# Softmax sums on GpSimd, routing products and early lo parts on VectorE, new TensorE costs in the planner

## The chip, the cores and the metric

One core of a Trainium2 chip runs the kernel. Its engines work side by side, each through its own list of instructions in order: TensorE (PE; its weight loads are shown apart as PEld), VectorE (DVE), ScalarE (ACT), GpSimd (POOL) and SyncE (SP), which here issues transfers. The metric is the device time of one execution in microseconds, the median of several. The profile comes from one further execution, and all times read from it count from the start of its span.

## What is computed

Attention over 4 batches of 8 heads with 576 rows of 64 numbers, causal in blocks of 64 rows; its output, 2304 rows of 512, goes through a mixture of 8 experts with two chosen for each row, and then through a second one with one chosen for each row.

```python
# attention, per batch and head (S = 576, D = 64)
scores = q @ k.T / sqrt(64);  scores[block_i < block_j] = -1e9     # blocks of 64
attn = exp(scores - scores.max(-1))
attn = attn / (attn.sum(-1) + 1e-9)
x = (attn @ v) -> [2304, 512]
# first mixture (E = 8, F = 1024)
logits = x @ w_gate + log1p(exp(x @ w_noise)) * noise
top2, top2_w = the two largest of 8, softmax over them
out[mask] += top2_w * (relu(x[mask] @ w1[e]) @ w2[e])              # for each expert e
# second mixture
logits = x @ w_gate + modality_bias[modality_id];  e_idx = argmax
out[mask] = gate_w * (relu(x[mask] @ w1[e]) @ w2[e])
```

All inputs and outputs are 32-bit floats.

## The kernel before, in words

Every matmul of the large products is done in three passes of a rounded 32-bit type: an operand is split into a high part (a copy with rounding, ScalarE) and a low part (the rest, a subtraction). For the weights these tiles are called wh and wl (from raw, the loaded tile; kld, qld and other attention buffers serve as raw for the earliest), for rows of x xth and xtl, for the hidden layer hh and hl (kept in tiles kp), for the attention's probabilities PTh and PTl.

**Attention** runs in 16 pairs, each of two heads of one batch (`NPAIR`). The steps of a pair have names: T and K/Q (transposes and splits of q and k), S0 to S8 (scores, TensorE, banks ps), M (row maxima nm, VectorE), E (exponentials p with their sums ss, ScalarE), B (transposes of p on TensorE, banks pt), H and L (PTh and PTl), V (values, banks pa), C, X and XC (transposes back into xu, ScalarE). R, R1 and R2 make the factors of the rows: R adds the two halves of the last sum (1 column), R1 adds 1e-9 to all nine, R2 takes four reciprocals of at most 5 columns into rr; all three are VectorE's. GpSimd multiplies finished rows by them (x and LH, from xu and rr, of an earlier pair) and splits v (vs: a copy and a subtraction). Where nothing else is said, a step stands once in a pair.

What sets the order there is a planner at build time. The table `SCHED` (L19) gives a pair's length, 14.5 us, and for each step a due time in it. The loop takes, among the next steps of TensorE, ScalarE and VectorE whose predecessors (`before`, L1220) are done by the planner's own clocks, the one that can start first, within 0.15 us the one due first. The clocks run by costs: `dve_cost`, `pe_cost` (L83 to L91), `act_cost`, `pool_cost`, and a lag from one engine to the next (`lag`, L1216). A step of GpSimd is not in these lists; it is emitted behind the step that makes it ready.

**Routing** of the first mixture (`route`, L643) is a chain of small VectorE steps that is laid between the attention's steps (`aside`): after pair 7 and after pair 11 for two parts of the rows, after pair 15 for the last. It makes one-hot tables (`hot_b`, `hot_a`, L284; tiles sl_ob, sl_oa, and their product sl_ov with five values for each slot) which a matmul sums into lists of rows (`lists`, L295); `slot_ids` turns these into the row numbers by which an indirect DMA gathers each expert's rows. A flag `early` stands for the lists of the first experts, `ids1` for all. `hot_a` is given the engine for its product: GpSimd for the first two routings (128x2000 each), VectorE for the last.

**The first expert's first weights** are split while attention still runs (`Stage.split`, called at fixed times 110, 124, ... plus 11 us; and steps JS of the hidden layer behind the last pair, two of four on GpSimd). Then `run` goes through the experts: `mm1` for each of eight blocks of the hidden layer (banks ph), `mm2` for each 128 rows (banks py), and between them one split of the next expert's weights each (lists `ea` and `eb` say on which engine), the transposes of the next rows (px, xth, xtl), the rows' transfers and a `filler`, which carries out what is left of the routing. VectorE's dots of the rows with the gate weights of the second mixture (zero, from yr or py and wgb) make the next gate.

A helper class (`Timed`) records every operation, so each row of the trace carries its line, L71; tiles tell the rows apart.

The names that the change touches: `pe_cost` L83, `hot_a` L284, `lists` L295, `Stage.split` L450, `route` L643, R, R1 and R2 L975 to L990, `last_route` and `routes` L1127 to L1140, `S_` L1183, `OFF`, `engine`, `lag` and `before` L1206 to L1223, `emit` L1259, `earliest` L1280, the splits at fixed times L1309, `run` L1372.

Of the kernel before, what the change touches and what calls it, by code (L numbers as in the profile page):

```python
# [30 lines left out]
def moe_kernel(tc, q, k, v, w_gate, w_noise, noise, w1, w2, mod_id, w_gate2, mod_bias, m2w1, m2w2, out):  # L31
# [54 lines left out]
    def pe_cost(name, o, i, kw):  # L86
        n = cols_of(o)
        dt = i.dtype
        if name == "transpose":
            return n * .00084  # L90
        return 2 * max(cols_of(i) * .00084, n * .00084) if dt == F32 else n * .000417 + .0145 * (clk["base"] is None)  # L91
# [12 lines left out]
    with ExitStack() as top:  # L104
# [177 lines left out]
        made = [0]  # L282

        def hot_a(pool, a, n, a0, na, vals, eng):  # L284
# [5 lines left out]
            eng.tensor_tensor(ov, bc(oa[:, :, None, :], [128, n, NV, na]), bc(vals[:, :, :, None], [128, n, NV, na]), op=OP.mult)  # L290
            made[0] = clk["pool"] if eng is gps else 0
            yield .3
            return ov

        def lists(pl, ob, ov, n, first=True, last=True):  # L295
            yield "pe", made[0]
# [134 lines left out]
        class Stage:  # L431
# [18 lines left out]
            def split(s, eng):  # L450
# [5 lines left out]
                for x, raw in enumerate(parts):  # L456
                    act.activation(hi[:, m * x:m * x + m], raw, AF.Copy)
                    eng.tensor_sub(lo[:, m * x:m * x + m], raw, hi[:, m * x:m * x + m].bitcast(F32))
# [184 lines left out]
        def route(b0, nb, slow):  # L643
# [99 lines left out]
            for b in range(nb):  # L743
                n = slice(10 * b, 10 * b + 10)
                ob = yield from hot_b(rt, bl[:, n], 10)
                ov = yield from hot_a(rt, a[:, n], 10, 0, NA1, va[:, n], gps if slow else vec)
# [38 lines left out]
        with ExitStack() as ph:  # L785
# [70 lines left out]
            def pair(p):  # L856
# [118 lines left out]
                def R():  # L975
                    vec.tensor_add(st["ss"][:, 8:9], st["ss"][:, 8:9], st["ss"][:, 9:10])

                def R1():
                    vec.tensor_scalar(st["ss"][:, 0:9], st["ss"][:, 0:9], 1e-9, None, op0=OP.add)
# [12 lines left out]
                f.update(S8=S8, M8=M8, N8=N8, E8=E8, R=R, R1=R1, R2=R2)  # L992
# [134 lines left out]
            def last_route():  # L1127
                yield from route(B - 1, 1, False)
# [6 lines left out]
            def routes(i):  # L1135
                if i < 2:
                    yield from route((B - 2) * i, B - 2 - i, True)
# [7 lines left out]
            def first_steps():  # L1145
# [37 lines left out]
                def S_(i):  # L1183
                    stage.split(vec if i in (2, 3) else gps)
                    fetch_b(1)
# [21 lines left out]
            OFF.update(N8=OFF["M8"] + .1, R1=OFF["R"] + .1, R2=OFF["R"] + .2)  # L1207
            kinds = dict(T="pe", M="pe", H="act", R="act", S="act", L="dve", V="dve")

            def engine(n):  # L1210
                if n[0] == "J":
                    return kinds[n[1]]
                if n[0] in "TSBV" or n in ("X0", "X1"):
# [3 lines left out]
            lag = {"pe": .26, "act": .15, "dve": .13}  # L1217
# [4 lines left out]
                      "R": E_, "BT": ["E8"], "HT": ["BT"], "LT": ["HT"], "VX": ["L0", "VS"], "CX": ["VX"], "V0": L_ + ["VS"], "V1": L_ + ["VS"],  # L1222
# [443 lines left out]
```

## Time and profile before

| | us |
|---|---|
| median of 3 runs | 1021.34 (1020.36 to 1021.66) |
| profiled execution, whole time | 1020.32 |
| its span in the profile | 1018.5 |
| TensorE busy | 960.6 (94%) |
| VectorE busy | 733.8 (72%) |
| GpSimd busy | 528.5 (52%) |
| ScalarE busy | 519.0 (51%) |
| mean granted clock of TensorE | 0.985 of full |

The span is cut into stretches by what runs in it. From 30 to 144 us it is attention alone, from 144 to 265 attention with routing steps between, from 265 to 292 the hidden layer of expert 0, from 292 to 320 its second layer and the beginning of expert 1, from 320 to 400 the rest of expert 1, and from there the other experts of the first mixture, its gate and the second mixture. In a table of stretches each engine has its busy time and, in brackets, its number of instructions; a stretch less the busy time is the engine's idle time there. In a timeline the first number is the start, the second the length, then engine, line, operation, output <- inputs with their shapes, and at the end in square brackets the idle time ahead of it and whose instruction ended it. Instructions of one group that follow each other are put together (x4), and a group's length is then that of all.

### The profile page before, as it was taken

The page shows a single profiled execution, that of the slowest core. Times are in us where ns is not written, and L with a number is a line of the kernel's source. Part 1 is how long each engine was busy: PE and PEld are TensorE (multiplying, and loading weights), DVE is VectorE, ACT ScalarE, POOL GpSimd, SP SyncE. Part 2 cuts the span into 40 slices and gives each one's busy share as a digit, 9 for nine tenths or more (in the row PEclk, how much of TensorE's full clock was granted, in tenths as well). Part 3 has the DMA queues.
Part 4 walks back from the last instruction along what each step waited for, and adds up shares of the span by engine and source line. Part 5 has one row for each costly group of instructions (what it writes and reads, how often), then busy time and mean ns, then how long its engine had stood idle before and what let it go on. Part 6 is the DMA issues. An engine that isn't in the chain of part 4 may idle for free.

```text
span 1018.5 us, 17480 instructions
## 1 busy us (share of the span) xinstructions
PE 960.6 (94%) x6058; PEld 867.4 (85%) x6058; DVE 733.8 (72%) x1766; ACT 519.0 (51%) x1156; POOL 528.5 (52%) x387
## 2 busy tenths in 40 slices
PE   7999998898996999999999999999999989999995
PEld 5888887788886888998989898998979878999995
DVE  6888779989878596839396775939799876545541
ACT  5888887878653234433334333333325455555551
POOL 5123142373265649968485775847477345333231
PEclk8999999999997999999999999999999999999998
DMA  5556644322055636656374654625177867766620
GB/s 124 110 148 180 190 112 112 83 70 87 24 188 145 197 62 169 165 136 135 90 149 104 134 122 118 125 77 92 45 187 187 272 206 237 228 214 230 196 98 12
DMA packets 158257, 141.59 MB, mean 139 GB/s; under 512 B 76233, under 2 KB 124745, under 8 KB 158034
## 3 DMA queue, kind: packets, MB, share of 16 engines
q1 hardware_dynamic: 140098, 107.18, 35.6%
q0 software_dynamic: 18064, 33.23, 15.8%
q8 instruction: 50, 0.82, 0.4%
q14 instruction: 45, 0.37, 0.1%
HBM read 112.54 MB, written 28.36 MB: 138 GB/s over the span
## 4 chain that ended last, share of the span: by engine, by line
PE 74%; DVE 13%; issue 4%; ACT 3%; POOL 2%; DMA 2%; SPq 1%; POOLq 0%; DVEq 0%; ACTq 0%
PE ph L71 29%; PE py L71 25%; PE pt L71 8%; PE ps L71 6%; PE pa L71 4%; PE px L71 2%; POOL wl L71 1%; DVE ss L71 1%; DVE kp L71 1%; DVE zero L71 1%; DVE nm L71 1%; DVE PTl L71 1%; DMA wgb<-WG2T 1%; DMA xr<-X,ids 1%; DVE wl L71 1%
## 5 line engine op out<-in xcount | busy, mean ns | idle before, releaser
L71 POOL TENSOR_TENSOR wl<-raw,wh 128x1024 fp32r<-128x1024 f32 x88 | 226.8, 2624 | 112.4 <-ACT wh L71 98.2
L71 PE MATMUL ph<-xth,wh 128*128 128x320 f32 (+2 forms) x800 | 243.1, 304 | 12.5 <-DVE kp L71 12.5
L71 PE MATMUL ph<-xtl,wh 128*128 128x320 f32 (+2 forms) x800 | 241.9, 302 | 0.0
L71 PE MATMUL ph<-xth,wl 128*128 128x320 f32 (+2 forms) x800 | 241.8, 302 | 0.0
L71 DVE SCALAR_TENSOR_TENSOR zero<-py,gts,wgb 128x512 f32<-128x512 f32 x304 | 227.5, 748 | 8.6 <-issue 0.4
L71 PE MATMUL py<-wh,kp 128*128 128x512 f32 x496 | 166.9, 397 | 0.0
L71 PEld LDWEIGHTS ph<-xth,wh 128*128 128x128 f32 x800 | 153.3, 192 | 14.1 <-DVE kp L71 13.4
L71 PEld LDWEIGHTS ph<-xtl,wh 128*128 128x128 f32 x800 | 153.3, 192 | 0.7
L71 PEld LDWEIGHTS ph<-xth,wl 128*128 128x128 f32 x800 | 153.3, 192 | 0.0
L71 ACT ACTIVATE wh<-raw 128x1024 fp32r<-128x1024 f32 x144 | 150.8, 1053 | 0.7 <-DMA raw<-in_moe_w_dram 0.7
L71 ACT ACTIVATE yr<-py,gts 128x512 f32<-128x512 f32 x60 | 41.3, 689 | 147.0 <-PE py L71 104.4
L71 PEld LDWEIGHTS py<-wh,kp 128*128 128x128 f32 x496 | 93.3, 188 | 18.2
L71 DVE SCALAR_TENSOR_TENSOR hl<-ph,hh 128x320 fp32r<-128x320 f32 (+2 forms) x100 | 46.5, 466 | 80.6 <-ACT hh L71 80.3
L71 PE MATMUL ps<-kh,kp 128*128 128x256 f32 (+5 forms) x320 | 98.6, 349 | 2.5 <-POOL kp L71 1.0
L71 PE MATMUL py<-wl,kp 128*128 128x512 f32 x248 | 96.8, 391 | 0.0
L71 PE MATMUL py<-wh,hh 128*128 128x512 f32 x232 | 94.0, 405 | 0.0
L71 PE MATMUL py<-wl,hh 128*128 128x512 f32 x232 | 90.7, 391 | 1.4 <-POOL wl L71 1.4
L71 DVE TENSOR_TENSOR xtl<-px,xth 128x512 fp32r<-128x512 f32 x58 | 40.0, 690 | 71.3 <-ACT xth L71 71.0
L71 PE MATMUL py<-wh,hl 128*128 128x512 f32 x232 | 90.9, 392 | 0.0
L71 ACT ACTIVATE hh<-ph 128x320 fp32r<-128x320 f32 (+2 forms) x100 | 41.8, 418 | 95.4 <-PE ph L71 92.2
L71 POOL DMA_INDIRECT xr<-X,ids x55 | 58.1, 1057 | 62.2 <-PE px L71 47.4
L71 DVE TENSOR_TENSOR wl<-raw,wh 128x1024 fp32r<-128x1024 f32 x56 | 70.0, 1259 | 27.8 <-ACT wh L71 27.6
(252 smaller groups left out, 1861.4 us busy)
## 6 DMA issues: line engine op xcount, KB each, us to landing
raw<-in_moe_w_dram SPq DMA_DIRECT2D x144, 512.0 KB, 4.2
X<-zero SPq DMA_DIRECT2D x13, 512.0 KB, 3.6
kld<-in_k_dram SPq DMA_DIRECT2D x32, 128.0 KB, 2.7
qld<-in_q_dram SPq DMA_DIRECT2D x32, 128.0 KB, 2.8
vld<-in_v_dram SPq DMA_DIRECT2D x32, 128.0 KB, 2.7
X<-x SPq DMA_DIRECT2D x16, 256.0 KB, 2.3
xs<-in_moe_w_dram SPq DMA_DIRECT2D x4, 512.0 KB, 4.2
wgb<-WG2T POOLq DMA_DIRECT2D x1, 2048.0 KB, 9.0
```

The lines of the kernel that those rows point to most:

```text
L71: return f(*a, **kw)
```

## The change

- **Sums.** R adds both halves of the last sum and then 1e-9 to all nine, on GpSimd (R1 is gone). It is emitted as soon as the last exponential of its pair is. R2, the reciprocals, takes the due time that R had, and waits for R with the lag of GpSimd, 0.3 us.
- **Routing.** The product sl_ov is VectorE's in every routing, in two halves where it has more than 200 columns of one-hots. `lists` no longer reckons with GpSimd's clock.
- **Early lo parts.** The lo parts of weights that are split in attention buffers (`pre`) are written in halves of 512 columns. The first expert's lo parts are VectorE's, and in `run` all of them until the slot table of all experts (`ids1`) is there; from then on the lists `ea` and `eb` hold as before.
- **Planner's costs.** A 32-bit matmul costs 0.224 us whatever its size, a matmul of the rounded type its columns by 0.417 ns and 13.5 ns more (attention had no such addition, later stages had 14.5 ns), a transposed column 0.85 ns rather than 0.84. The table of due times itself is unchanged.

The core of the diff; what is left out passes on the same arguments or edits the table `before` so that R2 stands behind R.

```diff
@@ -87,8 +87,8 @@
         if name == "transpose":
-            return n * .00084
-        return 2 * max(cols_of(i) * .00084, n * .00084) if dt == F32 else n * .000417 + .0145 * (clk["base"] is None)
+            return n * .00085
+        return .224 if dt == F32 else n * .000417 + .0135
...
-        def hot_a(pool, a, n, a0, na, vals, eng):
+        def hot_a(pool, a, n, a0, na, vals):
...
-            eng.tensor_tensor(ov, bc(oa[:, :, None, :], [128, n, NV, na]), bc(vals[:, :, :, None], [128, n, NV, na]), op=OP.mult)
-            made[0] = clk["pool"] if eng is gps else 0
-            yield .3
+            m = -(-n // 2) if n * na > 200 else n
+            for c in range(0, n, m):
+                s = slice(c, min(c + m, n))
+                vec.tensor_tensor(ov[:, s], bc(oa[:, s, None, :], [128, s.stop - c, NV, na]),
+                                  bc(vals[:, s, :, None], [128, s.stop - c, NV, na]), op=OP.mult)
+                yield .3
             return ov
 
         def lists(pl, ob, ov, n, first=True, last=True):
-            yield "pe", made[0]
+            yield "pe", 0
...
-                    eng.tensor_sub(lo[:, m * x:m * x + m], raw, hi[:, m * x:m * x + m].bitcast(F32))
+
+                    k = 512 if parts[0] is pre else m
+                    for c in range(0, m, k):
+                        d = slice(m * x + c, m * x + c + k)
+                        eng.tensor_sub(lo[:, d], raw[:, c:c + k], hi[:, d].bitcast(F32))
...
-                ov = yield from hot_a(rt, a[:, n], 10, 0, NA1, va[:, n], gps if slow else vec)
+                ov = yield from hot_a(rt, a[:, n], 10, 0, NA1, va[:, n])
...
                 def R():
-                    vec.tensor_add(st["ss"][:, 8:9], st["ss"][:, 8:9], st["ss"][:, 9:10])
-
-                def R1():
-                    vec.tensor_scalar(st["ss"][:, 0:9], st["ss"][:, 0:9], 1e-9, None, op0=OP.add)
+                    gps.tensor_add(st["ss"][:, 8:9], st["ss"][:, 8:9], st["ss"][:, 9:10])
+                    gps.tensor_scalar(st["ss"][:, 0:9], st["ss"][:, 0:9], 1e-9, None, op0=OP.add)
...
                 def S_(i):
-                    stage.split(vec if i in (2, 3) else gps)
+                    stage.split(vec)
...
-            OFF.update(N8=OFF["M8"] + .1, R1=OFF["R"] + .1, R2=OFF["R"] + .2)
+            OFF.update(N8=OFF["M8"] + .1, R2=OFF.pop("R"))
...
+                if n in ("R", "VS"):
+                    return "pool"
...
-            lag = {"pe": .26, "act": .15, "dve": .13}
+            lag = {"pe": .26, "act": .15, "dve": .13, "pool": .3}
...
-                fin[p, n] = clk["pool" if n == "VS" else engine(n)]
+                fin[p, n] = clk[engine(n)]
+                if n in E_ and all((p, x) in fin for x in E_):
+                    emit(p, "R", t)
...
-                at(110 + 14 * i + 11, lambda: stage.split(gps))
+                at(110 + 14 * i + 11, lambda: stage.split(vec))
...
-                        stage.split(eb[fs.index(f) % len(eb)])
+                        stage.split(eb[fs.index(f) % len(eb)] if "ids1" in flags else vec)
...
-                            stage.split(ea[left[1] % len(ea)])
+                            stage.split(ea[left[1] % len(ea)] if "ids1" in flags else vec)
```

What this moves is read from the order of the instructions on each engine, at three places.

VectorE in the fourth pair, from the last split of the keys (kp) on. Before, the sums (ss) and the reciprocals (rr) stand ahead of PTh:

```order
L71 SCALAR_TENSOR_TENSOR kp_158<-pt,kp_156 64x8x64 x2
L71 TENSOR_TENSOR ss<-ss 128x1
L71 TENSOR_SCALAR ss<-ss 128x9
L71 RECIPROCAL rr_161<-ss 64x5
L71 RECIPROCAL rr_161<-ss 64x4
L71 RECIPROCAL rr_161<-ss 64x5
L71 RECIPROCAL rr_161<-ss 64x4
L71 TENSOR_TENSOR PTh<-pt,PTh 64x128
L71 TENSOR_REDUCE nm<-ps 128x1
L71 TENSOR_TENSOR PTl<-pt,PTh 128x512 x2
L71 TENSOR_REDUCE nm<-ps 128x1
L71 TENSOR_TENSOR PTl<-pt,PTh 128x512 x2
```

After:

```order
L71 SCALAR_TENSOR_TENSOR kp_158<-pt,kp_156 64x8x64 x2
L71 TENSOR_TENSOR PTh<-pt,PTh 64x128
L71 TENSOR_REDUCE nm<-ps 128x1
L71 TENSOR_TENSOR PTl<-pt,PTh 128x512 x2
L71 TENSOR_REDUCE nm<-ps 128x1
L71 TENSOR_TENSOR PTl<-pt,PTh 128x512 x2
L71 TENSOR_REDUCE nm<-ps 128x1
L71 TENSOR_TENSOR PTl<-pt,PTh 128x128
L71 TENSOR_TENSOR PTl<-pt,PTh 128x384
L71 TENSOR_TENSOR PTl<-pt,PTh 128x512
L71 TENSOR_REDUCE nm<-ps 128x1 x2
L71 RECIPROCAL rr_161<-ss 64x5
```

The sums are gone from VectorE, PTh follows the keys at once, and the reciprocals stand behind the last lo parts.

GpSimd in the pair that follows, from one pair's x to the next's (vs is the split of v, LH a smaller piece of x). Before:

```order
L71 TENSOR_TENSOR x<-xu_164,rr_163 128x2x5x64
L71 CAST vs<-vld 128x10x64
L71 TENSOR_TENSOR LH<-xu_164,rr_163 128x2x5x16
L71 TENSOR_TENSOR vs<-vld,vs 128x10x64
L71 TENSOR_TENSOR x<-xu_165,rr_161 128x2x5x64
```

After:

```order
L71 TENSOR_TENSOR x<-xu_164,rr_163 128x2x5x64
L71 TENSOR_TENSOR vs<-vld,vs 128x10x64
L71 TENSOR_TENSOR LH<-xu_164,rr_163 128x2x5x16
L71 TENSOR_SCALAR ss<-ss 128x9
L71 TENSOR_TENSOR ss<-ss 128x1
L71 CAST vs<-vld 128x10x64
L71 TENSOR_TENSOR x<-xu_165,rr_161 128x2x5x64
```

The sum of nine columns stands behind x, vs and LH, the sum of one column (the next pair's) follows it, and the copy vs has moved ahead of x.

VectorE in expert 1's hidden layer, where the slot table is finished (pos_k, base, pc, then sl_a, sl_b, the gates g and the values vals of the last routing; kp is a block's low part). Before:

```order
L71 COPY base<-pos 128x8
L71 COPY pc<-pos_k 128x2x5
L71 TENSOR_SCALAR sl_a_4267<-pc 128x10
L71 TENSOR_SCALAR sl_a_4267<-sl_a_4267 128x10
L71 SCALAR_TENSOR_TENSOR sl_b_4268<-sl_a_4267,pc 128x10
L71 TENSOR_SCALAR big<-sl_a_4267 128x10
L71 TENSOR_TENSOR sl_a_4267<-sl_a_4267,big 128x10
L71 SCALAR_TENSOR_TENSOR sl_a_4267<-ek,sl_a_4267 128x2x5
L71 TENSOR_SCALAR d<-e_4234 128x5
L71 RECIPROCAL g<-d 128x5
L71 TENSOR_TENSOR g<-e_4234,g 128x5
L71 SCALAR_TENSOR_TENSOR kp_4286<-ph,kp_4286 128x384
```

After, at the same place in the list:

```order
L71 CAST vals<-g 128x2x5
L71 SCALAR_TENSOR_TENSOR kp_4294<-ph,kp_4294 128x384
L71 TENSOR_TENSOR wl<-raw,wh 128x1024
L71 TENSOR_TENSOR t_4310<-g,vals 128x10
L71 CAST vals<-t_4310 128x2x5
L71 TENSOR_TENSOR vals<-t_4310,vals 128x2x5
L71 TENSOR_TENSOR sl_ob<-lane,sl_b_4275 128x1280
L71 SCALAR_TENSOR_TENSOR kp_4325<-ph,kp_4325 128x384
L71 TENSOR_TENSOR wl<-raw,wh 128x1024
L71 TENSOR_TENSOR sl_oa<-lane,sl_a_4274 128x400
L71 TENSOR_TENSOR sl_ov<-sl_oa,vals 128x1000
L71 SCALAR_TENSOR_TENSOR kp_4351<-ph,kp_4351 128x384
```

The routing's small steps are some ten places earlier in the list, and lo parts of the weights (wl) stand between the blocks' low parts.

## Rows read from the trace of the kernel before

**Rows 1.** The page, section 1: busy time, share of the span, instructions

```profile
PE 960.6 (94%) x6058; PEld 867.4 (85%) x6058; DVE 733.8 (72%) x1766; ACT 519.0 (51%) x1156; POOL 528.5 (52%) x387
```

**Rows 2.** Stretches: length; busy (x) PE, PEld, DVE, ACT, POOL; clock; DMA; GB/s

```profile
30.00:144.00 114.00, 105.97 (x765) 96.65 (x763) 93.11 (x224) 95.38 (x298) 27.14 (x31) 1.00 0.57 155
144.00:265.00 121.00, 109.40 (x789) 98.62 (x789) 111.31 (x302) 94.95 (x296) 50.59 (x39) 0.99 0.30 79
265.00:292.00 27.00, 25.42 (x204) 23.87 (x203) 17.16 (x56) 15.60 (x43) 14.00 (x12) 1.00 0.21 59
292.00:320.00 28.00, 19.63 (x110) 17.00 (x108) 26.28 (x50) 11.74 (x18) 19.84 (x11) 0.92 0.84 238
320.00:336.00 16.00, 16.00 (x79) 15.18 (x80) 9.57 (x20) 4.36 (x7) 6.45 (x4) 0.82 0.22 69
336.00:400.00 64.00, 61.28 (x342) 55.24 (x340) 50.11 (x133) 20.98 (x35) 43.03 (x32) 0.97 0.56 149
400.00:1019.00 619.00, 600.00 (x3660) 542.14 (x3659) 406.73 (x936) 257.87 (x409) 352.35 (x206) 0.99 0.55 148
```

**Rows 3.** Waits of PE in 30:144: total us, times, longest us

```profile
PE pt L71 <- DVE PTh L71: 5.1, 6, 0.9
PE pt L71 <- DVE PTl L71: 1.7, 1, 1.7
```

**Rows 4.** Timeline of DVE, then PE, around 67 us: start, length, instruction, wait

```profile
65.89 1.06 DVE L71 TENSOR_TENSOR ss<-ss 128x1 f32<-128x1 f32 x1
67.05 0.57 DVE L71 TENSOR_SCALAR ss<-ss 128x9 f32<-128x9 f32 x1
67.72 0.75 DVE L71 RECIPROCAL rr<-ss 64x5 f32<-64x5 f32 x4
68.40 0.27 DVE L71 TENSOR_TENSOR PTh<-pt,PTh 64x128 fp32r<-64x128 f32 x1
...
68.72 0.65 PE L71 MATMUL pt<-ident,p 128*128 128x128 f32 x4 [0.87 <-DVE PTh L71]
...
131.64 0.65 PE L71 MATMUL pt<-ident,p 128*128 128x128 f32 x4 [0.87 <-DVE PTh L71]
```

**Rows 5.** Timeline of POOL in the same stretch, and its small scalar operation

```profile
65.67 1.26 POOL L71 TENSOR_TENSOR x<-xu,rr 128x640 f32<-128x640 f32 x1 [11.81 <-ACT xu L71]
...
67.97 1.56 POOL L71 TENSOR_TENSOR vs<-vld,vs 128x640 fp32r<-128x640 f32 x1
...
76.93 0.22 POOL L71 TENSOR_SCALAR mn<-midf 128x18 f32<-128x18 f32 x1
```

**Rows 6.** Timeline of DVE, POOL and PE in expert 1's hidden layer

```profile
304.35 4.66 DVE L71 TENSOR_TENSOR tp<-oh,pos 128x80 f32<-128x80 f32 x1
...
309.41 8.29 DVE L71 COPY base<-pos 128x8 f32<-128x8 f32 x1
...
310.14 7.52 POOL L71 TENSOR_TENSOR wl<-raw,wh 128x1024 fp32r<-128x1024 f32 x3
...
319.91 0.69 PE L71 MATMUL ph<-xth,wh 128*128 128x384 f32 x1 [8.37 <-DVE kp L71]
```

**Rows 7.** Groups by line and form: count, busy us, mean ns, idle before

```profile
L71 DVE TENSOR_TENSOR wl<-raw,wh 128x1024 fp32r<-128x1024 f32 x56 | 70.0, 1259 | 27.8 <-ACT wh L71 27.6
...
L71 DVE TENSOR_SCALAR ss<-ss 128x9 f32<-128x9 f32 x16 | 11.4, 713 | 2.3 <-ACT p L71 1.5
...
L71 DVE TENSOR_TENSOR ss<-ss 128x1 f32<-128x1 f32 x16 | 9.0, 565 | 0.3
...
L71 DVE TENSOR_TENSOR sl_ov<-sl_oa,vals 128x2000 bf16<-128x2000 bf16 x1 | 2.2, 2242 | 0.0
...
L71 DVE TENSOR_TENSOR wl<-qld,wh 128x512 fp32r<-128x512 f32 x2 | 1.4, 683 | 0.0
```

**Rows 8.** Timeline of DVE and PE, expert 1's other half

```profile
345.34 0.69 DVE L71 SCALAR_TENSOR_TENSOR zero<-yr,wgb 128x512 f32<-128x512 f32 x1 [6.58 <-DMA wgb<-WG2T]
...
358.75 0.39 PE L71 MATMUL ph<-xth,wh 128*128 128x256 f32 x1 [2.39 <-DVE kp L71]
```

More of the change, by code (lines that the diff above doesn't have):

```diff
@@ L280, in hot_b @@
             return ob
-        made = [0]
-        def hot_a(pool, a, n, a0, na, vals, eng):
+        def hot_a(pool, a, n, a0, na, vals):
             oa = pool.tile([128, n, na], BF16, name="sl_oa")
@@ L640, in moe_kernel, with route @@
         stage = Stage([j00, j10] + firsts + seconds)
-        def route(b0, nb, slow):
+        def route(b0, nb):
             C = 5 * nb
@@ L991, in pair @@
                     one(i)
-                f.update(S8=S8, M8=M8, N8=N8, E8=E8, R=R, R1=R1, R2=R2)
+                f.update(S8=S8, M8=M8, N8=N8, E8=E8, R=R, R2=R2)
                 blocks = [(n, i, j) for j, n0 in ((0, 0), (1, 9), (2, 16), (3, 22)) for n, i in enumerate(range(2 * j, 9), n0)]
@@ L1127, in last_route @@
             def last_route():
-                yield from route(B - 1, 1, False)
+                yield from route(B - 1, 1)
                 yield from slot_ids(rt, acc1, NA1, 64, pad1.rearrange("p e t -> p (e t)"), ids1, gts1)
@@ L1136, in routes @@
                 if i < 2:
-                    yield from route((B - 2) * i, B - 2 - i, True)
+                    yield from route((B - 2) * i, B - 2 - i)
                     yield from early(i)
@@ L1221, in moe_kernel @@
             before = {"TQ": [], "TK": [], "T4": ["TK"], "QH": ["TQ"], "QL": ["QH"], "KH": ["TK"], "KL": ["KH"], "A4": ["T4"], "D4": ["A4"],
-                      "R": E_, "BT": ["E8"], "HT": ["BT"], "LT": ["HT"], "VX": ["L0", "VS"], "CX": ["VX"], "V0": L_ + ["VS"], "V1": L_ + ["VS"],
-                      "C0": ["V0", "CX"], "C1": ["V1", "CX"], "X0": ["C0"], "X1": ["C1"], "XC0": ["X0", "R2"], "XC1": ["X1", "R2"], "R1": ["R"], "R2": ["R1"]}
+                      "BT": ["E8"], "HT": ["BT"], "LT": ["HT"], "VX": ["L0", "VS"], "CX": ["VX"], "V0": L_ + ["VS"], "V1": L_ + ["VS"],
+                      "C0": ["V0", "CX"], "C1": ["V1", "CX"], "X0": ["C0"], "X1": ["C1"], "XC0": ["X0", "R2"], "XC1": ["X1", "R2"], "R2": ["R"]}
             for i in blk:
@@ L1285, in earliest @@
                             return None
-                        t = max(t, fin[p - k, d] + (.3 if d == "VS" else 0 if d[0] in "FG" else lag[engine(d)]))
+                        t = max(t, fin[p - k, d] + (0 if d[0] in "FG" else lag[engine(d)]))
                 if n[0] in bank and e == "pe":
@@ L1524, in gates @@
                     ob = yield from hot_b(pool, bl[:, n], HN)
-                    ov = yield from hot_a(pool, a[:, n], HN, a0, na, vals2[:, n], vec)
+                    ov = yield from hot_a(pool, a[:, n], HN, a0, na, vals2[:, n])
                     yield from lists(pl, ob, ov, HN, i == 0, i == 1)
@@ L1570, in moe_kernel @@
                     ob = done(hot_b(r1, bl[:, n], 10))
-                    ov = done(hot_a(r1, a[:, n], 10, 0, NT2, vals.rearrange("p c k v -> p (c k) v")[:, n], vec))
+                    ov = done(hot_a(r1, a[:, n], 10, 0, NT2, vals.rearrange("p c k v -> p (c k) v")[:, n]))
                     done(lists(pl, ob, ov, 10, i == 0, i == B - 1))
```

## The prediction

> **What bounds the kernel now.** I read the page's line of busy times first [rows 1]: TensorE is busy 960.6 of 1018.5 us, so only 57.9 us can be won by waits, plus what a lowered clock costs. VectorE is busy 733.8 us, GpSimd 528.5. So I read the stretches next [rows 2], to see where the waits lie. TensorE's idle time is the stretch less its busy time: 8.0 us in 30 to 144 (attention without routing), 11.6 in 144 to 265 (attention with the routing steps between), 1.6 in 265 to 292 (first hidden layer of expert 0), 8.4 in 292 to 320 (second layer of expert 0, hidden layer of expert 1), 2.7 in 336 to 400. From 400 on TensorE waits for 19 of 619 us, with steps that the change hardly touches. So the change is worth what it does ahead of 400.
>
> Who ends the waits is the next view. In 30 to 144 it is VectorE: seven waits, 6.8 us [rows 3]. The instructions show why [rows 4, 5]. Two tiny sums, of 1 and 9 columns, take 1.06 and 0.57 us there; they start while GpSimd works on x (65.67 to 66.93) and vs. The four reciprocals follow, and only then PTh, whose end frees the transposes' bank: TensorE waits 0.87 us, up to PTh's end. The same wait recurs from 68.72 to 131.64 in five pairs, 15.73 us apart. At 319.91 the pattern is the same and larger [rows 6]: a copy of 8 columns takes 8.29 us on VectorE, and GpSimd has three 1024-column lo parts in a row under it (7.52 us). TensorE has filled its three banks and waits 8.37 us for kp. After that its clock is lowered: 0.82 of full in 320 to 336 [rows 2].
>
> **The change, part by part.** The sum is made against the profiled run, 1020.32 us (span 1018.5 and 1.8 around it); the median of the three runs is 1.0 above it.
>
> Sums on GpSimd, attention without routing. Per pair VectorE loses 0.565 and 0.713 us (means [rows 7]), and the order puts the reciprocals behind five maxima and all lo parts instead of ahead of PTh. PTh then starts some 2.4 us earlier (1.06 + 0.57 + 0.75), more than the 0.87 to 1.7 us that TensorE waits. TensorE's order there is unchanged, so no other step is ahead of the bank. All seven waits go: -6.8. ScalarE is next, busy 95.4 of 114 us, so I leave 0.8 us for new waits: **-6.0**. On GpSimd the two sums are new. The nearest row is a scalar operation of 18 columns, 0.22 us [rows 5], so 0.44 us a pair beside 27 busy us in 114; bounds 0.2 and 2.6 us a pair (the latter if they wait there for the port as on VectorE, twice 1.3). They cost nothing as long as they end before the reciprocals. The sum of 9 stands behind x of two pairs earlier, vs and LH; by the rows GpSimd is through with these at 69.5, and in the new place VectorE reaches the reciprocals about 8 us after PTh's 68.4, so some 6 us later. That cover is what the slow rival takes away.
>
> Attention with routing (144 to 265). VectorE is busy 111.3 of 121 us: this stretch is its own. Taken from it: seven pairs of sums, 7 x 1.28 = 9.0 us. Put on it: two routing products at 2.24 us each [rows 7] (4.5; each in two halves), eight half lo parts of the early weights at 0.68 (5.5), and the third routing product with its one-hots and slot numbers. The planner now runs these ahead of the last pair's reciprocals, where before they stood in 265 to 292, which is TensorE's: 2.24 plus some 4 us, 6 us in all. Net +7 us of VectorE work. On the other side, GpSimd loses 4 lo parts and 2 products, so there is less to wait behind, and TensorE's 11.6 idle us and the 0.99 clock (some 1.2 us) are the margin from which gains come. Bounds: -6 (half of that idle time goes, as in the stretch before) and +8 (all of the net work is exposed). Since VectorE is at 92% there, I take a value nearer to the bad end than to the good: **+1.5**.
>
> The Trainium skill speaks against this part: "SBUF — State Buffer", section "Who interferes with whom", says that a VectorE instruction with two SBUF inputs contends with a GpSimd instruction that reads SBUF, and that the later one waits until the first is finished. By that rule each moved lo part and product can be held by x or vs, and with GpSimd's share of the stretch the sum would be about 3 us worse. The sums' 1.06 us beside x agree with it; no row of before shows a lo part on VectorE beside x.
>
> Lo parts of expert 0's second weights (265 to 292): two more of the four go to VectorE, 4 x 0.68 = 2.7 us. It has 9.8 idle us there and loses about 6 us of routing. TensorE's 1.6 idle us go for the most part: **-1.1**.
>
> Expert 1's hidden layer (292 to 336). The lo parts up to the slot table (eight of 1024 columns) move from GpSimd to VectorE at 1.26 us each. GpSimd then has no long instruction there, and the copy of 8 columns takes what one reciprocal of 5 columns does, 0.75 / 4 = 0.19 us [rows 4]: 8.1 us less, and the row tp 4.4 us less [rows 6]. VectorE's work up to the fourth kp: I count from the first xtl along the order. By uncontended durations the first kp is written after 13.1 us, the second after 16.8, the third after 20.2, the fourth after 21.8; TensorE's blocks (2.1 us, the first 8.4 us after xtl) need them at 14.8, 16.8, 18.9 and 22.3. So one wait of 1.3 us is left; with the rest I say 1.5. Gone: 8.4 idle, and the clock: at 0.82 over 16 us the work lost is 2.9 us, of which 2.6 follows that wait. 8.4 + 2.6 - 1.5: **-9.5**; bounds -11.5 and -3 (if each of the eight lo parts pushes VectorE by as much again, 5 to 6 us of waiting come back).
>
> Expert 1's other half (336 to 400). TensorE waits 2.39 us for kp behind sixteen gate dots, which can start only once the gate weights are loaded (345.34) [rows 8], and the clock of 0.97 costs 1.9 us, of which 1.4 I put to this wait. With the slot table some 8 us earlier the load is earlier too, though TensorE is then earlier as well by 9.5; but the order puts 13 dots ahead of the first kp instead of 17, 4 x 0.73 = 2.9 us less. That covers the wait: -3.8, less 0.5 for a new one: **-3.3**; bounds -4 and 0.
>
> The planner's new TensorE costs: in 30 to 144 TensorE's order is the old one, at the start one block of transposes is earlier, past 400 the same matmuls follow each other. Cost nothing; bounds -1 and +3 for the chain of gates, whose steps fall elsewhere.
>
> Sum: -6.0 + 1.5 - 1.1 - 9.5 - 3.3 = -18.4. 1020.3 - 18.4 = 1001.9 for a run like the profiled one, and 1.0 more for the median: **1003 us**.
>
> **The rivals.**
> 1. VectorE becomes the bound with routing: its 111.3 busy us grow by 7 and the wait per pair stays, so +8 instead of +1.5; it comes late into expert 1 and half of that gain (4 us) goes too. 1003 + 6.5 + 4 = 1013. For it: 92% busy, in-order. Against: GpSimd's 3.5 and 2.4 us instructions are gone, and tiny operations were what was held. Also here: the rule of the page on the shared port, as a mechanism of these rows (x and vs, 1.26 and 1.56 us each pair, hold the moved products), at 1006 alone. Chance 0.24.
> 2. The planner's more exact costs and the free port help with routing too (-6 instead of +1.5): 995. For it: every wait there was ended by VectorE as well. Chance 0.18.
> 3. The change does not do what it says on the steady pairs: ScalarE, 84% busy, takes the wait over, and nothing of the 6.0 comes: 1009. Against: its order is unchanged and it waits for TensorE itself. It lies in the same band as a half of rival 1. Chance 0.08.
> 4. Slower: the sums on GpSimd come too late. They stand behind x, which waits for ScalarE's xu. VectorE works in order, so reciprocals that wait hold the maxima, kl and kp behind them, hence the next scores. The price is the time by which they are late, once per pair for 14 pairs; it decides from 18.4 / 14 = 1.3 us a pair beyond the cover of some 6 us. At 2.5 us (the two longest waits of such a sum) the time is 1003 + 35 = 1038. Chance 0.05.
>
> **How the numbers follow.** Forecast (996 to 1008) 0.45; rival 1 0.24, rival 2 0.18, rival 3 0.08, rival 4 0.05. A range of 991 to 1015 takes in rivals 1, 2 and 3 and the bounds of single terms; it leaves out rival 4 and the case that several terms fall to one end. What a measurement can tell from no change is 0.2%, 2 us. Rival 1 with the bad bounds of two other terms reaches no change: 0.04. Faster 0.90, within 0.2% 0.04, slower 0.06.
>
> **What would show it.** Right: x starts on GpSimd about 14.9 us apart instead of 15.73 between 60 and 130; VectorE's longest instruction ahead of 340 is below 3 us; TensorE has no wait over 2 us in 290 to 340, and its clock stays near 1.00 there; expert 0's second layer starts at 287 to 288 instead of 292.5, and the gain at 400 is some 18 us and stays to the end. Wrong: reciprocals that wait for GpSimd's sums (rival 4), VectorE over 95% busy in the routing stretch with pairs 17 us apart or more (rival 1), waits for ScalarE's PTh in steady pairs (rival 3), or a gain ahead of 400 that is given back at the gate chain near 800.

## The result and the profile after

The kernel became slower: 1028.23 us median (1026.05 to 1032.48, 8 runs) beside 1021.77 (8 runs); the ratio is 1.006, 95% interval 1.0036 to 1.0083. The forecast was 1003 us, range 991 to 1015. The profiled execution has a span of 1025.9 us, 7.4 more than before.

The stretches of [rows 2], now of the kernel after (length; busy time and count of PE, PEld, DVE, ACT, POOL; clock; DMA share; GB/s):

```profile
30.00:144.00 114.00, 113.20 (x837) 105.47 (x836) 88.85 (x225) 101.80 (x316) 35.10 (x52) 1.00 0.61 167
144.00:265.00 121.00, 101.88 (x703) 89.77 (x702) 112.82 (x296) 84.78 (x267) 30.81 (x41) 0.96 0.27 69
292.00:320.00 28.00, 26.39 (x151) 23.40 (x150) 24.81 (x64) 15.15 (x25) 3.52 (x3) 1.00 0.79 225
320.00:336.00 16.00, 14.56 (x83) 12.47 (x82) 7.43 (x17) 4.20 (x7) 3.27 (x8) 1.00 0.60 217
336.00:400.00 64.00, 60.93 (x339) 54.93 (x338) 51.34 (x137) 22.72 (x36) 49.83 (x30) 0.97 0.56 128
```

Attention without routing is better than forecast: TensorE has 837 matmuls done in 30 to 144 where it had 765. With routing it is worse: 703 where it had 789, and the clock is 0.96 where it was 0.99. Expert 1's hidden layer is as forecast, clock 1.00 and no long wait.

Since the work in a stretch of equal time differs, I compare the same piece of work. Each mark below is the start of a piece on TensorE, read from its timeline. "Old costs" is the run `no_cost` below, the whole change without the planner's new numbers; "two parts" is the run `sums_ids1`.

| mark on TensorE | before | after | old costs | two parts | forecast |
|---|---|---|---|---|---|
| keys of the eighth pair | 106.6 | -9.2 | -7.3 | -9.8 | |
| keys of the eleventh pair | 156.0 | -11.9 | -8.4 | -12.5 | |
| expert 0, second layer | 292.6 | +1.7 | -2.1 | -12.2 | -5.6 |
| expert 1, second layer | 334.0 | -7.2 | -11.7 | -20.8 | |
| expert 1's other half, second layer | 367.5 | -10.3 | -13.4 | -24.8 | |
| the expert after it, hidden layer | 379.9 | -5.4 | -7.7 | -17.9 | -18.4 |
| first expert of the second mixture, hidden layer (start of the gate chain) | 766.9 | -7.7 | -9.6 | -19.9 | -18.4 |
| a hidden layer behind the gate chain | 845.1 | +7.2 | -9.6 | -19.2 | -18.4 |
| last expert, second layer | 997.2 | +7.3 | -9.6 | -19.1 | -18.4 |

So 7.7 us are won by 767, and 14.9 are given back in the next 78, in the chain of gates, to which the prediction had given -1 to +3. TensorE's waits there (total, times, longest), first of before, then of after:

```profile
PE px L71 <- DMA xr<-X,ids: 3.1, 3, 1.7
PE ph L71 <- DVE kp L71: 1.7, 2, 1.1
PE pt L71 <- DVE sl_ov L71: 1.6, 1, 1.6
PE pt L71 <- DVE g_oh L71: 0.5, 1, 0.5
```

```profile
PE ph L71 <- DVE hl L71: 4.6, 1, 4.6
PE pt L71 <- DVE sl_ov L71: 4.2, 1, 4.2
PE pt L71 <- DVE g_oh L71: 3.2, 1, 3.2
PE px L71 <- DMA xr<-X,ids: 3.0, 3, 1.6
PE ph L71 <- DVE kp L71: 0.5, 2, 0.3
```

The first wait of after is a new one. Its timeline on VectorE, GpSimd and TensorE:

```profile
768.10 6.12 DVE L71 TENSOR_TENSOR wl<-raw,wh 128x1024 fp32r<-128x1024 f32 x1
774.14 0.41 DVE L71 SCALAR_TENSOR_TENSOR hl<-ph,hh 128x256 fp32r<-128x256 f32 x1
...
766.83 1.58 POOL L71 DMA_INDIRECT LG<-yg,ids  x1 [0.30 <-issue]
767.87 5.26 POOL L71 TENSOR_TENSOR wl<-raw,wh 128x1024 fp32r<-128x1024 f32 x2
...
774.61 0.58 PE L71 MATMUL ph<-xth,wh 128*128 128x256 f32 x1 [4.60 <-DVE hl L71]
774.99 0.42 PE L71 MATMUL ph<-xtl,wh 128*128 128x256 f32 x1
```

VectorE's lo part starts 0.23 us after GpSimd's two, and ends 1.1 us after both (773.13). The block's low part hl stands behind it, and TensorE waits. It is the picture of [rows 6] at another place. The second matmul behind the wait takes 0.42 us where such a one took 0.28: the clock is lowered, 0.91 in 760 to 840. In the kernel before the same piece reads:

```profile
767.31 2.99 POOL L71 TENSOR_TENSOR wl<-raw,wh 128x1024 fp32r<-128x1024 f32 x1
770.46 1.78 POOL L71 DMA_INDIRECT xr<-X,ids  x1 [0.16 <-issue]
772.55 1.58 POOL L71 DMA_INDIRECT X<-yr,ids  x1 [0.30 <-issue]
774.44 1.56 POOL L71 DMA_INDIRECT LG<-yg,ids  x1 [0.30 <-DVE zero L71]
775.49 5.33 POOL L71 TENSOR_TENSOR wl<-raw,wh 128x1024 fp32r<-128x1024 f32 x2
...
774.44 1.25 DVE L71 TENSOR_TENSOR wl<-raw,wh 128x1024 fp32r<-128x1024 f32 x1
```

There GpSimd has a gather (xr) more between its lo parts, comes to its pair 1.05 us after VectorE began, and VectorE's lo part takes 1.25 us.

The two other waits that grew are of the same kind. TensorE waits there for two small products of VectorE, g_oh and sl_ov. After, with the lo parts that GpSimd has beside them:

```profile
801.06 2.35 POOL L71 TENSOR_TENSOR wl<-raw,wh 128x1024 fp32r<-128x1024 f32 x1 [3.69 <-ACT wh L71]
801.24 2.33 DVE L71 TENSOR_TENSOR g_oh<-g_oh,g_msk 128x144 bf16<-128x144 bf16 x1
...
824.96 2.51 POOL L71 TENSOR_TENSOR wl<-raw,wh 128x1024 fp32r<-128x1024 f32 x1 [1.70 <-ACT wh L71]
825.19 2.67 DVE L71 TENSOR_TENSOR sl_ov<-sl_oa,vals 128x360 bf16<-128x360 bf16 x1
```

And before:

```profile
800.94 0.30 DVE L71 TENSOR_TENSOR g_oh<-g_oh,g_msk 128x144 bf16<-128x144 bf16 x1
801.90 2.39 POOL L71 TENSOR_TENSOR wl<-raw,wh 128x1024 fp32r<-128x1024 f32 x1 [4.72 <-ACT wh L71]
...
820.92 0.52 DVE L71 TENSOR_TENSOR sl_ov<-sl_oa,vals 128x360 bf16<-128x360 bf16 x1
821.03 2.66 POOL L71 TENSOR_TENSOR wl<-raw,wh 128x1024 fp32r<-128x1024 f32 x1 [1.82 <-ACT wh L71]
```

After, GpSimd is first by 0.18 and 0.23 us, and the products take 2.33 and 2.67 us; before, VectorE is first by 0.96 and 0.11 us, and they take 0.30 and 0.52. By TensorE's starts of the same pieces the 14.9 us lie at these three places: 7.7 us ahead at 766.9, after is 0.2 behind at 790.3, 3.8 at 816.5 and 7.2 at 845.1. So 7.9 go at the wait for hl, 3.6 at that for g_oh and 3.4 at that for sl_ov, each with what the lowered clock behind it costs (in 760 to 840 the clock was 1.00 before).

### The profile page after: what moved, and what is told of

It is laid out like the page before. It is cut to its first block, busy times and chain, and to the rows that moved or that the text cites. A ratio compares the mean times of both kernels' runs of the same rounds, so it can differ in the third digit from the quotient of the medians.

```text
span 1025.9 us, 17473 instructions
## 1 busy us (share of the span) xinstructions
PE 966.2 (94%) x6058; PEld 871.4 (85%) x6058; DVE 732.9 (71%) x1761; ACT 518.0 (50%) x1156; POOL 491.0 (48%) x400
## 4 chain that ended last, share of the span: by engine, by line
PE 57%; issue 5%; DVE 4%; POOL 4%; DMA 2%; ACT 1%; POOLq 0%; SPq 0%; ACTq 0%
PE ph L71 28%; PE py L71 25%; PE px L71 2%; POOL wl L71 2%; DVE wl L71 1%; PE pt L71 1%; PE ps L71 1%; POOL X L71 1%; DMA xr<-X,ids 1%; POOL LG L71 0%; POOL xr L71 0%; DMA LG<-yg,ids 0%; PE pa L71 0%; DMA raw<-in_moe_w_dram 0%; ACT wh L71 0%
## 5 line engine op out<-in xcount | busy, mean ns | idle before, releaser
L71 POOL TENSOR_TENSOR wl<-raw,wh 128x1024 fp32r<-128x1024 f32 x80 | 207.0, 2618 | 107.0 <-ACT wh L71 92.8
L71 DVE SCALAR_TENSOR_TENSOR zero<-py,gts,wgb 128x512 f32<-128x512 f32 x296 | 221.6, 749 | 8.2
L71 PE MATMUL py<-wh,kp 128*128 128x512 f32 x496 | 169.0, 401 | 3.1 <-DVE zero L71 3.1
L71 DVE TENSOR_TENSOR wl<-raw,wh 128x1024 fp32r<-128x1024 f32 x64 | 84.2, 1323 | 28.6 <-ACT wh L71 28.4
L71 DVE TENSOR_TENSOR xtl<-px,xth 128x512 fp32r<-128x512 f32 x58 | 40.0, 690 | 78.5 <-ACT xth L71 78.4
```

What stands on the lines that cost most here:

```text
L71: return f(*a, **kw)
```

## The experiments

For all runs, the marks of the table above; "routing" is the time from the eighth pair's keys to expert 0's second layer, "chain" that from 766.9 to 845.1.

| run | median us | ratio to before (95%) | routing | chain |
|---|---|---|---|---|
| before | 1021.8 | | 185.9 | 78.2 |
| after | 1028.2 | 1.006 (1.0036 to 1.0083) | 196.9 | 93.0 |
| sums_only | 1010.7 | 0.988 (0.984 to 0.992) | 183.4 | 78.1 |
| ids1_only | 1010.8 | 0.987 (0.983 to 0.992) | 187.1 | 78.3 |
| prod_only | 1026.9 | 1.004 (1.003 to 1.006) | 196.1 | 78.3 |
| split_only | 1033.8 | 1.011 (1.007 to 1.015) | 197.0 | 78.4 |
| costs_only | 1037.6 | 1.015 (1.013 to 1.017) | 196.7 | 94.3 |
| costs_late | 1034.9 | 1.014 (1.010 to 1.017) | 185.9 | 95.3 |
| one_ns | 1032.9 | 1.011 (1.008 to 1.014) | 185.9 | 93.1 |
| no_cost | 1011.3 | 0.991 (0.989 to 0.993) | 191.1 | 78.2 |
| no_split | 1026.6 | 1.005 (1.004 to 1.007) | 195.7 | 84.3 |
| chain_vec | 1025.3 | 1.004 (1.002 to 1.005) | 196.3 | 88.5 |
| sums_ids1 | 1004.1 | 0.983 (0.981 to 0.985) | 183.5 | 78.8 |
| sums_ids1_cost | 1021.1 | 0.999 (0.997 to 1.002) | 192.9 | 88.1 |

A warning on single traces: up to the gate chain `chain_vec` is the same program as after, and its marks in attention differ from those by 2 to 3 us. Smaller differences between the marks of two traces are not read as effects.

**The parts alone.** My first theory: VectorE is the limit while routing runs, and the moved products and lo parts eat what the sums win.

```diff
 # sums_only: before, with only this (and its planner entries)
-                    vec.tensor_add(st["ss"][:, 8:9], ...); vec.tensor_scalar(st["ss"][:, 0:9], ...)
+                    gps.tensor_add(st["ss"][:, 8:9], ...); gps.tensor_scalar(st["ss"][:, 0:9], ...)
```

> The kernel before with one part of the change: the softmax sums on GpSimd. Marks are starts on TensorE: the second layer of expert 0 (292.6 us before, 294.3 with the whole change), the second layer of expert 1 (334.0 and 326.8), the hidden layer of the seventh expert of the row (648.2 and 641.0), and the length of the gate chain from the hidden layer at 766.9 to that at 845.1 (78.2 us before, 93.0 with the whole change). Theory (VectorE is the limit while routing runs, and what the other parts put on it ate the gain): the steady pairs take 14.5 us and the gain of some 11 us at the eleventh pair is kept, expert 0's second layer starts at 279 to 285. Rival (the sums come late on GpSimd once routing runs there, VectorE waits for them): the gain is lost again in the routing stretch, start at 290 or later, with waits of the reciprocals for GpSimd of over 2 us in several pairs. For the gate chain: if it hangs on the time at which lo parts of GpSimd and VectorE meet, its length may come out anywhere from 76 to 95; if it hangs on the planner's new costs it stays at 78.

Expert 0's second layer starts at 280.3, the steady pairs take 14.5 to 14.6 us, and all 12.2 us are kept through the routing. The theory holds; the sums on GpSimd come in time. The wait for PTh [rows 3] is gone; what is left in 30 to 144:

```profile
PE pt L71 <- ACT xs L71: 0.7, 1, 0.7
PE pt L71 <- DVE PTl L71: 0.5, 1, 0.5
```

```diff
 # prod_only: before, with only this
-                ov = yield from hot_a(rt, a[:, n], 10, 0, NA1, va[:, n], gps if slow else vec)
+                ov = yield from hot_a(rt, a[:, n], 10, 0, NA1, va[:, n])     # vec, in halves
```

> The kernel before with the routing products on VectorE alone, in halves. Theory (VectorE is the limit in the routing stretch): 4.5 us of moved products, of which at least 3 reach TensorE: expert 0's second layer starts at 295 to 299 instead of 292.6. Rival (GpSimd's products of 3.5 us held VectorE's small steps by as much as they save): within 1 us of 292.6. The marks behind it shift by the same; the gate chain as in the run of the sums.

302.1: 9.5 us later. Ahead of this mark three products are moved (two of the first routing, one of the second), not the two that the expectation counts: 6.7 us at 2.24 each [rows 7]. Here they took 10.1 us on VectorE; one half, beside a lo part of GpSimd, took 3.37 us, where a free one took 1.19. At the last pair's keys, with two products done, TensorE is 8.1 us later. The direction of the theory is right, its size too small.

```diff
 # split_only: before, with only this (and the halves of 512 columns)
-                    stage.split(vec if i in (2, 3) else gps)
+                    stage.split(vec)
-                at(110 + 14 * i + 11, lambda: stage.split(gps))
+                at(110 + 14 * i + 11, lambda: stage.split(vec))
```

> The kernel before with expert 0's first-layer lo parts on VectorE alone (in halves of 512 columns). Theory (VectorE is the limit in the routing stretch): 5.5 us more on VectorE there, of which 3 to 6 reach TensorE, and VectorE waits for ScalarE's high parts in front of each: expert 0's second layer starts at 295 to 299. Rival (lo parts on GpSimd held VectorE about as much): within 1 us of 292.6.

303.4: 10.9 us later. The edit moves more than the expectation counts: beside the eight half lo parts (5.5 us at 0.68 each, 8.3 us here, as GpSimd held some of them) also four halves of the second layer's weights, 2.7 us. At the last pair's keys, with the eight done, TensorE is 7.5 us later. TensorE's waits in 150 to 304 show where a part goes, to PTh and PTl, which stand behind the lo parts on VectorE; before, these two were 9.2 us together in 150 to 293:

```profile
PE pt L71 <- DVE PTh L71: 9.8, 5, 2.7
PE pt L71 <- DVE PTl L71: 4.4, 7, 2.4
```

```diff
 # ids1_only: before, with only this, and the same for ea
-                        stage.split(eb[fs.index(f) % len(eb)])
+                        stage.split(eb[fs.index(f) % len(eb)] if "ids1" in flags else vec)
```

> The kernel before with only the rule that lo parts are VectorE's until the slot table is there. Theory (the eight-column copy was held by three lo parts of GpSimd): nothing changes up to 292.6, the waits of 8.4 us go, expert 1's second layer starts at 323 to 328 instead of 334.0, and the gain of 6 to 10 us is still there at the hidden layer at 648.2. Rival (VectorE's own lo parts push the blocks' low parts as far): 331 to 335. Gate chain: 78 us if the planner's new costs made it long, anything from 76 to 95 if the time of meeting does, and then the total can be anywhere from 1012 to 1027.

No change up to 292.7, expert 1's second layer at 327.8, and 9.5 us won at 648. The two rows that were held in [rows 6] are now these:

```profile
306.77 0.24 DVE L71 TENSOR_TENSOR tp<-oh,pos 128x80 f32<-128x80 f32 x1
...
307.40 0.16 DVE L71 COPY base<-pos 128x8 f32<-128x8 f32 x1
```

4.66 and 8.29 us have become 0.24 and 0.16, with nothing else changed on these instructions than what runs on GpSimd: the copy was held by GpSimd's three lo parts. In all four runs the gate chain takes 78 us.

**The gate chain.** I held the collision at 768 to be an accident of the time at which the work arrives there.

```diff
 # costs_only: before, with only this
-            return n * .00084
-        return 2 * max(cols_of(i) * .00084, n * .00084) if dt == F32 else n * .000417 + .0145 * (clk["base"] is None)
+            return n * .00085
+        return .224 if dt == F32 else n * .000417 + .0135
```

> The kernel before with only the planner's new TensorE costs. Theory (the long gate chain of the whole change is a collision of lo parts at one moment, 768 us, and the costs have no part in it): marks within 3 us of before, gate chain (hidden layer at 766.9 to hidden layer at 845.1) 78 us, total 1018 to 1025. Rival (the costs move the chain's steps against TensorE's): gate chain 85 to 95 us, total 1028 to 1038.

The theory fell. The planner's numbers alone give the long chain, 94.3 us, with the same wait of 4.6 us for hl, and they lose 10.8 us in the routing besides. In attention without routing they win: the pairs are 14.57 us apart from the sixth on, though the sums stay on VectorE. The rows there:

```profile
94.63 0.16 DVE L71 TENSOR_TENSOR ss<-ss 128x1 f32<-128x1 f32 x1
95.02 0.17 DVE L71 TENSOR_SCALAR ss<-ss 128x9 f32<-128x9 f32 x1 [0.24 <-ACT p L71]
...
95.79 1.26 POOL L71 TENSOR_TENSOR x<-xu,rr 128x640 f32<-128x640 f32 x1
```

GpSimd's x starts 0.6 us behind the sums, where in [rows 4, 5] it began 0.2 us ahead of them, and 1.06 and 0.57 us have become 0.16 and 0.17. So the wait of the steady pairs goes by the order alone too.

```diff
 # chain_vec: after, with VectorE for the lo parts that meet at 768
-                        stage.split(eb[fs.index(f) % len(eb)] if "ids1" in flags else vec)
+                        stage.split(eb[fs.index(f) % len(eb)] if "ids1" in flags and j is not seconds[0] else vec)
```

> The whole change, but the four lo parts of the first expert of the second mixture (second-layer weights) are all VectorE's, where two of the four were GpSimd's. Theory (VectorE's lo part at 768.1, 6.1 us long, was held by two lo parts of GpSimd in a row, the wait of 4.6 us for hl followed, then a lowered clock and later gates): everything up to 759 as with the whole change, the gate chain 78 to 84 us instead of 93.0, total 1013 to 1019. Rival (the chain is long because its steps stand elsewhere): 90 us or more, total 1025 or more.

Between the two. The waits of TensorE for hl and g_oh are gone (the first hidden layer of the chain takes 12.0 us where it took 18.1), but a wait of 4.3 us for gathered rows follows at its end, and the chain takes 88.5 us. More is lost behind that mark, at a clock of 0.74 in 840 to 860: from 766.9 to the last expert's second layer this trace, taken on the slowest of the ten runs, loses 15.2 us, after 15.0. So the collision is the cause of the first 6 us, but without it as much is lost at other places; by the medians 3.0 us are won, with overlapping intervals.

```diff
 # costs_late: before; the new numbers only where clk["base"] is None, behind attention
-            return n * .00084
-        return 2 * max(cols_of(i) * .00084, n * .00084) if dt == F32 else n * .000417 + .0145 * (clk["base"] is None)
+            return n * (.00085 if clk["base"] is None else .00084)
+        if clk["base"] is None:
+            return .224 if dt == F32 else n * .000417 + .0135
+        return 2 * max(cols_of(i) * .00084, n * .00084) if dt == F32 else n * .000417
```

> The kernel before with the new TensorE costs only behind attention (13.5 instead of 14.5 ns on each matmul, and the 32-bit ones). Theory (that millisecond-long sum of 1 ns errors alone shifts the filler's steps against the blocks, and so the order in which GpSimd has gathers and lo parts): no change up to 292.6, gate chain 90 us or more, total 1032 to 1038. Rival (the attention part of the costs does it, by the clock that it hands on): gate chain 78 us, total 1020 to 1024.

No change up to 292.9, chain 95.3: as the theory had it.

```diff
 # one_ns: before, with one number
-        ... n * .000417 + .0145 * (clk["base"] is None)
+        ... n * .000417 + .0135 * (clk["base"] is None)
```

> The kernel before with one number of the planner changed: 13.5 instead of 14.5 ns added to each matmul behind attention. In the order of instructions this moves, ahead of the gate chain, one gather of rows (xr) on GpSimd from between two lo parts to ahead of both. Theory (that place is what makes the chain long: with nothing between its two lo parts GpSimd runs them in a row, and VectorE's lo part, begun under the first, lasts until both are through): a lo part of about 6 us on VectorE, a wait of 4.5 us for hl, gate chain (hidden layer at 766.9 to hidden layer at 845.1) 90 to 96 us instead of 78.2, total 1030 to 1040. Rival (the other new numbers, of transposes and 32-bit matmuls, are needed for it): gate chain 76 to 82 us, total 1018 to 1025.

One nanosecond in the estimate of a matmul costs 11 us. What it moves on GpSimd between 380 and 800 is a gather, from between two lo parts to ahead of both. VectorE's order changes too, at several places from 329 on and in the chain, so that the gather alone was not tested. Before:

```
L71 DMA LG<-yg,ids 2944x9
L71 DMA xr<-X,ids 128x512 x2
L71 DMA X<-yr,ids 3072x512
L71 TENSOR_TENSOR wl<-raw,wh 128x1024
L71 DMA xr<-X,ids 128x512
L71 DMA X<-yr,ids 3072x512
```

And with the one number:

```
L71 DMA LG<-yg,ids 2944x9
L71 DMA xr<-X,ids 128x512
L71 DMA X<-yr,ids 3072x512
L71 DMA xr<-X,ids 128x512
L71 TENSOR_TENSOR wl<-raw,wh 128x1024
L71 DMA X<-yr,ids 3072x512
```

Its trace, on VectorE, GpSimd and TensorE:

```profile
773.82 6.06 DVE L71 TENSOR_TENSOR wl<-raw,wh 128x1024 fp32r<-128x1024 f32 x1
...
773.56 5.23 POOL L71 TENSOR_TENSOR wl<-raw,wh 128x1024 fp32r<-128x1024 f32 x2
...
780.27 0.58 PE L71 MATMUL ph<-xth,wh 128*128 128x256 f32 x1 [4.54 <-DVE hl L71]
```

VectorE's lo part begins 0.26 us after GpSimd's pair and is held to its end, where in before it began 1.05 us ahead of it. The two later collisions are there too, with waits of 3.3 us for g_oh and 4.2 us for sl_ov.

**Combinations.**

```diff
 # no_cost: after, with pe_cost of before
+            return n * .00084
+        return 2 * max(cols_of(i) * .00084, n * .00084) if dt == F32 else n * .000417 + .0145 * (clk["base"] is None)
```

> The whole change with the planner's TensorE costs of before. Theory (the new costs make the gate chain long, by the order that they give GpSimd's and VectorE's lo parts there): the gate chain (hidden layer at 766.9 to hidden layer at 845.1) takes 77 to 80 us instead of 93.0; the marks up to 759 within 5 us of those of the whole change, total 1009 to 1017. Rival (the parts together make it long too, by when they arrive): 85 us or more, total 1020 or more.

Chain 78.2, median 1011.3: the whole change with the old numbers is 1% faster than before. The sign of the result is that of the planner's numbers.

```diff
 # no_split: after, with the early lo parts as before
-                    stage.split(vec)
+                    stage.split(vec if i in (2, 3) else gps)
-                at(110 + 14 * i + 11, lambda: stage.split(vec))
+                at(110 + 14 * i + 11, lambda: stage.split(gps))
...
```

> The whole change without moving the lo parts of expert 0's first layer to VectorE. Theory (these lo parts are the dearest part: 10.9 us at expert 0's second layer when moved alone): that layer starts at 284 to 288 instead of 294.3; total 1010 to 1020, by what the gate chain does. Rival (with the sums gone VectorE has room for them): 292 to 294.

293.1: hardly better, as the rival said, so the parts' losses don't add. That products and costs fill the place which the lo parts leave is my reading, not shown.

```diff
 # sums_ids1: before, with the sums on GpSimd and the "ids1" rule, nothing else
```

> The kernel before with the two parts that won alone: the sums on GpSimd and lo parts on VectorE until the slot table is there; routing products, the lo parts of expert 0's first layer and the planner's costs as before. Theory (the two act in different stretches): 12 us earlier at expert 0's second layer, some 18 us at the hidden layer at 648.2, total 1001 to 1006 unless the gate chain meets the collision (then up to 15 more). Rival (both win the same time, that of the lists which come earlier): 1008 to 1012.

1004.1 us, ratio 0.983 (0.981 to 0.985), the fastest of all: the two winning parts add up, 12.2 us at expert 0's second layer and 8.6 more at expert 1's.

```diff
 # sums_ids1_cost: sums_ids1 with pe_cost of after
```

> The two winning parts with the planner's new costs: the change without the products and without expert 0's lo parts on VectorE. Theory (the products and lo parts are what fill VectorE, the costs only move the order): expert 0's second layer at 280 to 286, gate chain 88 us or more, total 1012 to 1022. Rival (new costs lose in the routing stretch by themselves, 12.9 us when alone): expert 0's second layer at 288 to 295.

291.9, as the rival said: the new numbers cost some 9 us in the routing even with neither products nor lo parts moved, and 9 in the chain. That chain lacks the first collision and has the two later ones, with waits of 5.0 us for g_oh and 4.2 us for sl_ov. What the costs do in the routing shows in the stretch from the eleventh pair to expert 0's second layer, first before, then costs_only:

```profile
156.00:292.60 136.60, 123.49 (x911) 112.43 (x909) 119.48 (x335) 100.04 (x309) 57.28 (x44) 0.99 0.28 76
```

```profile
149.90:299.40 149.50, 131.24 (x910) 117.15 (x909) 127.78 (x341) 100.26 (x312) 56.72 (x46) 0.94 0.27 71
```

For the same work TensorE has 5.2 us more idle time and, at a clock of 0.94 for 0.99, 7.8 us more busy time; VectorE's busy time is 8.3 us longer with the same GpSimd work. In that run three small routing steps of at most 80 columns (u, oh, vals) take 2.34, 2.14 and 2.22 us on VectorE; before, none of these tiles' steps took over 1.1 us. Each of the three begins 0.07 to 0.33 us behind a lo part of GpSimd (2.36 to 2.38 us) and lasts to its end or a little longer. Which of the moved steps starts it is not settled.

## Why the prediction was wrong

- **Sums in the steady pairs: right, and too small.** Forecast -6.0; at the eleventh pair after is 11.9 us ahead, and sums_only, with this part alone, 12.5. I priced only the wait of 0.87 us; the pair fell from 15.73 to 14.5 us, and a gain of some 4 us came with the first four pairs, which I had not looked at. Since the new costs alone shorten the later pairs nearly as much (costs_only), the runs do not say which of the two did it in the whole change. Rivals 3 and 4 did not come: the longest wait of the reciprocals for GpSimd's sum is 1.4 us.
- **Attention with routing: the mis-sized term.** Forecast +1.5 (and -1.1 behind it); the piece from the eighth pair on takes 10.9 us more after, 5.1 with the old costs. I had counted the moved work rightly (+7 net), but took most of it as hidden. Alone, 6.7 us of products cost 9.5 and 8.2 us of lo parts 10.9, some 1.3 to 1.4 times as much; at the last pair's keys it is 8.1 for 4.5 and 7.5 for 5.5. In these two runs GpSimd held some of the moved pieces, and TensorE's clock from the eleventh pair on was 0.94 and 0.95 where it was 0.99. In the whole change the halves that were moved up to the last pair ran free (0.69 and 1.20 us each); what makes up its 10.9 us was not told apart. Rival 1 (+8 instead of +1.5) described it, at a chance of 0.24.
- **Expert 1's hidden layer: right.** Forecast -9.5, measured -8.9 (from +1.7 to -7.2). The run with this part alone shows the cause; it wins 6.3 us here and the rest in the other half.
- **Expert 1's other half: the new wait was mis-sized.** The wait for kp of [rows 8] went, and 4.1 us with it up to the second layer (-6.1 at the hidden layer to -10.3). Then VectorE's dots, which I gave 0.5 us, hold TensorE for 3.1 us and the clock falls, to 0.83 in 366 to 376; 4.9 us are given back:

```profile
366.87 0.67 PE L71 MATMUL py<-wh,kp 128*128 128x512 f32 x1 [3.07 <-DVE zero L71]
```

  It stands so in two runs with the old costs too (no_cost 3.86 us, sums_ids1 3.9).

- **The planner's new TensorE costs: the step that failed.** "Cost nothing; bounds -1 and +3". They decide the result: 1028.2 with them, 1011.3 without, so a term that I had put at nothing measured 17 us. 14.9 us are lost in the gate chain, in three collisions of GpSimd's lo parts with VectorE, past 400, where I had said that the change hardly touches TensorE's waits. With the old costs the time would have lain in my range, with a gain of 10 us instead of the 18 forecast. I had compared TensorE's order up to 144 and past 400, but not in the routing stretch, where the new costs alone lose 10.8 us, nor GpSimd's order behind attention, where one gather changes its place ahead of a pair of lo parts. I named the sign that would prove me wrong (a gain given back near 800), but gave it no chance of its own. Its mechanism is the one that I had read in [rows 6] and used with the opposite sign.
- The sum: 25.8 us missed, of which 7.3 at expert 0's second layer (-5.6 against +1.7), 5.7 in expert 1 (-12.8 against -7.1) and 14.9 in the gate chain; 2.3 us that were won between 380 and 767 go off it.

The Trainium skill, "SBUF — State Buffer", section "Who interferes with whom", which I had weighed only for the routing, says that the port pair shared by VectorE and GpSimd is an exclusive lock and that the order of issue decides who blocks. The traces agree on who waits, and go further on how long: VectorE was held through two and three instructions of GpSimd in a row (6.12 us over 5.26, 8.29 over 7.52).

## What to carry to other kernels

A change of a planner's numbers is a change of every engine's order: compare the order on all of them, the helper engine included, and price the places where two engines that hold each other come within a microsecond. Work put on an engine that is 92% busy was not hidden here: it cost 1.3 to 1.8 times its uncontended duration, through what held it and through the waits and the clock of the engine behind it. And try the parts of a change apart: here two of five were worth 1.7%, and the others took more than that back.

## What the runs showed of the hardware

VectorE does not get its turn between GpSimd's instructions that follow each other without a gap: one lo part that begins 0.23 to 0.26 us after the first of two takes 6.06 to 6.12 us, while one that begins 1.05 us ahead takes 1.25 us. In no_split, where GpSimd's second lo part began 0.11 us behind the end of the first, VectorE's was through after 3.84 us. The order of start also decides for small steps: a product of 360 columns took 0.52 us when it began 0.11 us ahead of GpSimd's lo part, and 2.67 us when it began 0.23 us behind it. A start that differs by 1.3 us is thus worth 4.8 us on VectorE, one that differs by 0.34 us 2.2 us, and TensorE lost more by its clock (0.91 in 80 us). Three such places make up the 14.9 us of the long chain. Whether the two later ones follow from the first was not shown; sums_ids1_cost has them without it.
